# Attention and mixer on one core: the two tail blocks of the token weights in one load, the channel weights of eight steps in pairs of 1024 columns, and k of four units by rows

## The chip, the cores and the metric

The kernel runs on one core of one Trainium2 chip. The time is the device time of one execution in microseconds (us); before the change it is 796.07 (median of three runs, 795.79 to 797.73). Engines are named as the profile names them: PE is TensorE, DVE VectorE, ACT ScalarE, POOL GpSimd, SP SyncE; SPq is SyncE's DMA queue.

## What is computed

Linear attention followed by an MLP mixer. q, k and v have 8 batches, 8 heads, 576 positions and 64 columns.

```python
q_s = softmax(q, over the 64 columns)
k_s = softmax(k, over the 576 positions)
kv  = einsum('bhsd,bhse->bhde', k_s, v)
x   = einsum('bhsd,bhde->bhse', q_s, kv)      # to (8, 576, 512)
h   = relu(x^T @ w_tok1) @ w_tok2             # 576 -> 256 -> 576, over positions
u   = x + h^T
out = u + relu(u @ w_ch1) @ w_ch2             # 512 -> 1536 -> 512, over columns
```

Both softmaxes subtract their maximum first. The four weights are float64.

## The kernel before

A *unit* is one batch and one pair of heads; there are 32, four to a batch. The first eight (n = 0 to 7, `early`) run before the rest: for each, `softmax_k` and `softmax_q`, then `stage_qT`, `stage_kv` (L319, the product k^T v in `kvf`), `stage_y` (L387, w1f times q), `stage_h1` (L395, relu to `hh` and its low part `hl`, L403) and two times `stage_u` (L440 and L422: x and the second token product, in halves of 288 positions). `empty` then takes a half from PSUM into the high and low parts of u, `uh` and `ul` (L434, L435). A high part is the number rounded to the type `fp32r`, the low part what is left; a product of two such pairs takes three matmuls of the four.

After that the work goes by groups of 512 positions and, in each, by twelve steps f of 128 hidden columns: `ch1` (L477, relu(u @ w_ch1)) and `ch2` (L637, times w_ch2). The remaining units are woven in between by the table `put`; the last two groups go through a joint scheme of sums and products.

*k of an early unit.* It is loaded transposed, as `kt`. `softmax_k` takes the maximum over positions (L249), `exp` on ScalarE with that as bias (L253), and five transposes on PE (L256 four whole chunks, L259 the fifth) whose results ScalarE copies to `k_t` (L257, L260). *k of a late unit* (n above 8) is loaded in both layouts: the maximum goes into a column of `dg`, VectorE transposes it in squares of 32 (L265), a DMA writes it to DRAM as `row` (L267), a second one spreads it over all partitions as `mb` (L268), GpSimd subtracts (L278) and ScalarE takes exp (L279). Unit 8 is of a third kind: its maximum is spread by a product with `ones` (L272).

*Weights.* The float64 numbers come as pairs of 32-bit words. `load_weights` loads a block of 128 x 512 and `narrow` makes float32 of it: L201, L203, L204, L206 and L208 on VectorE and L202 on ScalarE; `split` then gives high (L125, ScalarE) and low (L126, VectorE) parts. `load_tok1` and `load_tok2` fill w1f and w2h/w2l, each with a smaller tail block (256 and 128 columns). `load_ch(f)` takes the two blocks of step f; steps 0 to 3 are called inside the loop over the early units, 4 to 11 inside the first channel steps.

What sets the order: the program is written with tiles, and a scheduler with a model of the time orders the instructions of each engine and of each queue; each engine then works its own list in order. `issue_after` (in the code `behind`) keeps a piece out of the lists until a named instruction is in. `early`, `stg` and `cv` are pools with two or three buffers, so a load waits until the buffer's last reader is done.

## Time and profile before

| | |
|---|---|
| median of three runs | 796.07 us |
| the profiled execution | 796.4 us |
| its span, first to last instruction | 794.5 us |
| TensorE's mean granted clock | 0.994 |
| PE busy | 779.0 us (98%) |
| DVE busy | 526.7 us (66%) |
| ACT busy | 326.5 us (41%) |
| POOL busy | 85.1 us (11%) |

The busy time says how much of the span an engine has work in hand. A share over the whole span hides stages, so the windows and timelines of a few stretches stand beside it. Where an engine is full, an instruction costs the time from its start to the next one's start, which is less than its own duration.

### The profile page before, as it was taken

The numbers are of one execution on the slowest core, as the hardware profiler recorded it, in microseconds if no ns is written. First come the engines' busy times: TensorE is split into PE (matmuls) and PEld (weight loads), VectorE is DVE, ScalarE is ACT, GpSimd is POOL, SyncE is SP. The second block draws the span as 40 slices with busy tenths as digits, with TensorE's granted clock in tenths as the row PEclk, the third lists the DMA queues.
The fourth block names the chain that finished last, engine by engine and source line by source line (L and its number), as shares of the span: only waits on it lengthen the run. The fifth ranks groups of instructions, "written<-read, shape, count | busy, mean of one in ns | idle before, by whom it ended". The sixth has DMA issues, their size and how long they took to land.

```text
span 794.5 us, 12177 instructions
## 1 busy us (share of the span) xinstructions
PE 779.0 (98%) x4478; PEld 650.9 (82%) x4478; DVE 526.7 (66%) x1208; ACT 326.5 (41%) x824; POOL 85.1 (11%) x77
## 2 busy tenths in 40 slices
PE   6899999999999999999999999999999999999998
PEld 6688888887888888888888888888888888888886
DVE  6899998897777445755575455564668558975441
ACT  6876544435553343344433434333434413232100
POOL 1000010003122111120201101111111000000020
PEclk8899999999999999999999999999999999999999
DMA  9753422334334221513141212313240000000011
GB/s 289 249 175 104 143 91 101 112 89 133 83 92 137 66 72 37 152 37 100 38 120 54 81 57 74 111 38 85 51 125 18 1 1 28 26 1 0 1 67 40
DMA packets 64786, 65.08 MB, mean 82 GB/s; under 512 B 41944, under 2 KB 45272, under 8 KB 64728
## 3 DMA queue, kind: packets, MB, share of 16 engines
...
## 4 chain that ended last, share of the span: by engine, by line
PE 87%; DVE 6%; ACT 3%; DMA 2%; issue 1%; POOL 1%; DVEq 0%; POOLq 0%; ACTq 0%
PE ps_o L637 30%; PE ps_h L477 26%; PE ps_h L586 7%; PE ps_h L387 6%; PE ps_h L422 5%; PE ps_h L637 4%; PE ps_h L319 2%; PE ps_h L456 2%; PE ps_h L395 1%; ACT q_t L292 1%; DMA q_t<-in_q 1%; PE ps_o L422 1%; DVE stack L374 1%; PE ps_o L387 1%; DVE st L286 0%
## 5 line engine op out<-in xcount | busy, mean ns | idle before, releaser
L637 PE MATMUL ps_o<-h2h,cw 128*128 128x512 f32 x768 | 226.6, 391 | 0.0
L477 PE MATMUL ps_h<-uh,cw 128*128 128x512 f32 x672 | 210.4, 393 | 0.0
L637 PEld LDWEIGHTS ps_o<-h2h,cw 128*128 128x128 f32 x768 | 142.5, 188 | 29.8 <-issue 0.4
L481 DVE SCALAR_TENSOR_TENSOR h2l<-ps_h,h2h 128x512 fp32r<-128x512 f32 x84 | 57.8, 688 | 153.2 <-ACT h2h L480 152.6
L477 PEld LDWEIGHTS ps_h<-uh,cw 128*128 128x128 f32 x672 | 123.7, 188 | 24.4 <-issue 0.4
L637 PE MATMUL ps_o<-h2l,cw 128*128 128x512 f32 x384 | 137.4, 390 | 0.0
L477 PE MATMUL ps_h<-ul,cw 128*128 128x512 f32 x336 | 130.9, 390 | 0.0
L480 ACT ACTIVATE h2h<-ps_h 128x512 fp32r<-128x512 f32 x84 | 49.9, 594 | 90.5 <-PE ps_h L477 80.0
L126 POOL TENSOR_TENSOR ql<-q_t,qh 128x640 fp32r<-128x640 f32 x24 | 39.5, 1647 | 425.6 <-ACT qh L125 390.4
L637 PEld LDWEIGHTS ps_o<-h2l,cw 128*128 128x128 f32 x384 | 72.0, 188 | 15.1
L477 PEld LDWEIGHTS ps_h<-ul,cw 128*128 128x128 f32 x336 | 63.1, 188 | 13.4
L374 DVE COPY stack<-cv_s 32x128 f32<-32x128 f32 (+1 forms) x264 | 55.7, 229 | 3.5 <-PE ps_h L456 0.6
L278 POOL TENSOR_TENSOR k_t<-k_t,mb 128x640 f32<-128x640 f32 x24 | 37.9, 1579 | 109.8 <-DMA mb<-row 78.7
L279 ACT ACTIVATE k_t<-k_t 128x640 f32<-128x640 f32 x24 | 17.7, 739 | 66.2 <-POOL k_t L278 66.2
L495 DVE TENSOR_TENSOR ul<-ps_h,ul 128x512 f32<-128x512 f32 x40 | 27.3, 687 | 24.1 <-PE ps_h L586 23.7
L374 ACT COPY stack<-cv_s 32x160 f32<-32x160 f32 (+1 forms) x120 | 37.4, 311 | 2.8 <-DVE cv_s L364 1.5
L434 ACT CAST uh<-ps_h 128x288 fp32r<-128x288 f32 (+8 forms) x84 | 25.1, 317 | 27.2 <-PE ps_h L456 22.6
L297 ACT ACTIVATE q_t<-q_t 128x640 f32<-128x640 f32 x28 | 20.7, 740 | 32.0 <-DVE q_t L296 31.9
L422 PE MATMUL ps_h<-w2h,hh 128*128 128x288 f32 x112 | 33.7, 302 | 0.0
L422 PE MATMUL ps_h<-w2l,hh 128*128 128x288 f32 x112 | 33.3, 298 | 0.0
L637 PE MATMUL ps_h<-cw 128*128 128x512 f32 x144 | 33.0, 389 | 0.0
L422 PE MATMUL ps_h<-w2h,hl 128*128 128x288 f32 x112 | 32.6, 296 | 0.0
...
## 6 DMA issues: line engine op xcount, KB each, us to landing
stg<-in_w SPq DMA_DIRECT2D x28, 512.0 KB, 3.3
...
mb<-row SPq DMA_DIRECT2D x23, 64.0 KB, 2.9
```

The costliest lines, as they stand in the source:

```text
L126: return lo_eng.tensor_tensor(lo, src, f32(hi), op=ALU.subtract).ins
L278: nc.gpsimd.tensor_tensor(kx, kx, mb.unsqueeze(1).broadcast_to([P, C1, P]), op=ALU.subtract)
L374: eng(stack[row : row + Q, h, 0:n, at : at + Q], turned[x * Q : (x + 1) * Q, 0:n, y * Q : (y + 1) * Q])
L387: nc.tensor.matmul(y[:, 0:TOK], a, w, start=(i == 0), stop=(i == len(mm) - 1))
L422: nc.tensor.matmul(t[:, 0:W], a, w, start=start and i == 0, stop=stop and i == len(mm) - 1)
L434: nc.scalar.copy(uh, src).ins,
L477: nc.tensor.matmul(t, cw[f][x][:, n, :], w, start=(i == 0), stop=(i == 3 * NJ - 1))
L480: nc.scalar.activation(hh, t, AF.Relu).ins,
L481: nc.vector.scalar_tensor_tensor(hl, t, 0.0, f32(hh), op0=ALU.max, op1=ALU.subtract).ins,
L495: nc.vector.tensor_tensor(t, a, b, op=op)
L586: nc.tensor.matmul(t, x(n), w[n], start=(n == 0 and i == 0), stop=(n == 1 and i == 2))
L637: nc.tensor.matmul(to, cw[f][x][:, n0 + n, :], w, start=(first and i == 0), stop=(last and i == 2))
```

## The change

1. **Joint tail.** The tail blocks of w_tok1 (256 columns) and w_tok2 (128) lie in one block and are loaded and narrowed together, 384 columns, into `tails`.
2. **Pairs.** Both blocks of a step f = 0 to 7 go into one raw tile `two` of 1024 columns with two DMAs and are narrowed and split by operations over 1024 columns. The loads are kept behind the issue of a unit's q load (`loaded`), the narrowing behind a unit's multiplication of q by its reciprocal sums (`ready`). Steps 8 to 11 stay as they were.
3. **k by rows for units 5 to 8.** `NATURAL = 5`: these are loaded in both layouts and take the path by `row` and `mb`. For 5 to 7 VectorE subtracts, behind the unit's `ready`, and the row's DMA stands behind the unit's q load; for 8 GpSimd subtracts. Their transposes on PE, and unit 8's product with `ones`, go.

```diff
-        if not u["early"]:
+        if n >= NATURAL:
             nc.sync.dma_start(t.rearrange("p c d -> p (c d)"), k[n])
...
+    def load_two(at, bt, loaded, begun):
+        pool, place = two[0]
...
+        raw = pool.tile([P, 2 * CW, 2], U32, name="two")
+        with behind(loaded):
+            for x, i in enumerate((at, bt)):
+                nc.sync.dma_start(raw[:, x * CW : (x + 1) * CW, :].rearrange("p n w -> p (n w)"), wt[i].bitcast(U32))
+        return narrow(raw, 2 * CW, None, place.tile([P, 2 * CW], U32, name="two_s"), begun)
+
+    def narrow(raw, n, out, s=None, begun=()):
...
-        load_weights(AT_TAIL, TOK, out=w1t)
+        load_weights(AT_TAIL, TOK + NT * TL, out=tails)
...
-        t = load_weights(AT_TAIL + 1, NT * TL).rearrange("p (n t) -> p n t", n=NT)
+        t = tails[:, TOK:].rearrange("p (n t) -> p n t", n=NT)
...
-    def load_ch(f):
+    def load_ch(f, loaded=(), begun=()):
+        if two:
+            t = load_two(AT_C1 + f, AT_C2 + f, loaded, begun).rearrange("p (x n m) -> p x n m", x=2, n=NJ)
+            hi, lo = (cw_rows[f][:, :, y : y + 3 : 2, :].rearrange("p n x m -> p x n m") for y in range(2))
+            narrowed[:] = [split(hi, lo, t, nc.vector)]
+            return
...
-        through = u["n"] > NE
+        through = u["n"] >= NATURAL
...
-        if u["early"]:
+        if u["n"] < NATURAL:
...
-            nc.sync.dma_start(row, dg[0:P:Q, Q : 2 * Q])
+            with behind(u["loaded"] if u["early"] else []):
+                nc.sync.dma_start(row, dg[0:P:Q, Q : 2 * Q])
...
-        nc.gpsimd.tensor_tensor(kx, kx, mb.unsqueeze(1).broadcast_to([P, C1, P]), op=ALU.subtract)
-        nc.scalar.activation(kx, kx, AF.Exp)
+        with behind(u["ready"] if u["early"] else []):
+            eng = nc.vector if u["early"] else nc.gpsimd
+            eng.tensor_tensor(kx, kx, mb.unsqueeze(1).broadcast_to([P, C1, P]), op=ALU.subtract)
+            nc.scalar.activation(kx, kx, AF.Exp)
...
+        u["ready"] = [ready] if u["n"] < NJ else [ready, taken]
...
-            load_ch(n - (NE - F_HEAD))
+
+            f = n - (NE - F_HEAD)
+            load_ch(f, units[min(2 * f + 5, NE - 1)]["loaded"], units[min(f + 5, NE - 1)]["ready"])
```

The new line numbers are 1 to 35 higher: L249 is L274, L387 L416, L395 L424, L403 L432, L422 L451, L440 L469, L477 L506, L201 to L208 are L221 to L228, L126 is L129, L278 is L306.

How the lists of three engines move. First PE, before, at the products of the last two early units (hh_1000 is unit 6's; kvf1_140 unit 7's): the products with unit 6's hh, then the first channel step.

```order
L440 MATMUL ps_o_1055<-qt_963,kvf1_140 128x288
L395 MATMUL ps_h_1048<-kvf1_140,ys_995 128x128 x2
L440 MATMUL ps_h_1065<-qt_963,kvf1_140 128x288
L422 MATMUL ps_h_1004<-w2h_102,hh_1000 128x288
L422 MATMUL ps_h_1004<-w2l_103,hh_1000 128x288
L422 MATMUL ps_o_1014<-w2h_102,hh_1000 128x288
L422 MATMUL ps_o_1014<-w2l_103,hh_1000 128x288
L477 MATMUL ps_h_1122<-uh0_105,cw0_122 128x512 x2
L477 MATMUL ps_h_1122<-ul0_109,cw0_122 128x512
```

Its last quarter, and behind it the rest of unit 6's products with hl_1001:

```order
L477 MATMUL ps_h_1122<-uh0_105,cw0_122 128x512 x2
L477 MATMUL ps_h_1122<-ul0_109,cw0_122 128x512
L422 MATMUL ps_h_1004<-w2h_102,hl_1001 128x288
L422 MATMUL ps_h_1004<-w2h_102,hh_1000 128x288
L422 MATMUL ps_h_1004<-w2l_103,hh_1000 128x288
```

PE in the new order, the end of unit 6's products (hl_964 is now its hl) and what follows:

```order
L451 MATMUL ps_o_977<-w2h_102,hh_963 128x288
L451 MATMUL ps_o_977<-w2l_103,hh_963 128x288
L451 MATMUL ps_o_977<-w2h_102,hl_964 128x288
L424 MATMUL ps_h_1001<-kvf1_147,ys_958 128x128 x2
L469 MATMUL ps_o_1008<-qt_926,kvf1_147 128x288
L469 MATMUL ps_h_1018<-qt_926,kvf1_147 128x288
L506 MATMUL ps_h_1067<-uh0_105,cw0_123 128x512 x2
L506 MATMUL ps_h_1067<-ul0_109,cw0_123 128x512
```

All products of unit 6, those with its hl too, now stand ahead of the first channel step, and unit 7's h1 and kvf products between them.

DVE before, up to hl of unit 6 (hl_1001):

```order
L435 TENSOR_TENSOR ul1_110<-ps_o_919,uh1_106 128x288
L435 TENSOR_TENSOR ul1_110<-ps_h_929,uh1_106 128x160
L206 SCALAR_TENSOR_TENSOR stg_1026<-stg_1026 128x512
L203 SCALAR_TENSOR_TENSOR cv_s_1039<-stg_1037,cv_s_1039 128x512
L435 TENSOR_TENSOR ul2_111<-ps_h_929,uh2_107 128x128
L208 TENSOR_TENSOR cv_s_1028<-stg_1026,cv_s_1028 128x512
L403 SCALAR_TENSOR_TENSOR hl_1001<-ps_o_997,hh_1000 128x256
L204 TENSOR_SCALAR stg_1037<-stg_1037 128x512
L206 SCALAR_TENSOR_TENSOR stg_1037<-stg_1037 128x512
L126 TENSOR_TENSOR cw0_122<-cv_s_1028,cw0_122 128x4x128
```

DVE now, up to hl of unit 6 (hl_964); two_914 and two_989 are the raw weights of f=1 and f=2:

```order
L228 TENSOR_TENSOR two_s_917<-two_914,two_s_917 128x1024
L223 SCALAR_TENSOR_TENSOR two_s_992<-two_989,two_s_992 128x1024
L464 TENSOR_TENSOR ul2_111<-ps_h_902,uh2_107 128x128
L353 TENSOR_SCALAR rs_947<-ps_o_936 128x1
L129 TENSOR_TENSOR cw0_123<-two_s_917,cw0_123 128x2x4x128
L224 TENSOR_SCALAR two_989<-two_989 128x1024
L432 SCALAR_TENSOR_TENSOR hl_964<-ps_o_960,hh_963 128x256
L354 RECIPROCAL rs_947<-rs_947 128x1
L226 SCALAR_TENSOR_TENSOR two_989<-two_989 128x1024
L221 TENSOR_SCALAR two_s_1033<-two_1030 128x1024
```

hl stands behind operations of 1024 columns of two steps, where there were some of 512 columns of one.

SP's queue before, from the weights of f=0 (stg_826, stg_837) past q of units 3 and 4 (q_t_448, q_t_549) to q of unit 5 (q_t_642) and the weights of f=1 on both sides of it (stg_941, stg_952):

```order
L193 DMA stg_826<-in_w 128x1024
L193 DMA stg_837<-in_w 128x1024
L153 DMA q_t_448<-in_q 128x640
L153 DMA q_t_549<-in_q 128x640
L150 DMA kt_t_640<-in_kt 128x640
L193 DMA stg_941<-in_w 128x1024
L180 DMA v_t_86<-in_v 128x4x64 x2
L182 DMA v_t_86<-in_v 32x2x64 x2
L153 DMA q_t_642<-in_q 128x640
L193 DMA stg_952<-in_w 128x1024
```

SP's queue now, at q of units 3 and 4 (q_t_446, q_t_547); stg_1310 is the first block of f=8:

```order
L184 DMA v_t_143<-in_v 128x4x64 x2
L186 DMA v_t_143<-in_v 32x2x64 x2
L197 DMA stg_1310<-in_w 128x1024
L157 DMA q_t_446<-in_q 128x640
L157 DMA q_t_547<-in_q 128x640
```

And a little further, from v of unit 4 to the broadcast of unit 5's maximum (mb_113):

```order
L184 DMA v_t_86<-in_v 128x4x64 x2
L186 DMA v_t_86<-in_v 32x2x64 x2
L154 DMA kt_t_726<-in_kt 128x640
L157 DMA q_t_640<-in_q 128x640
L293 DMA row_646<-dg_108 4x32
L211 DMA two_814<-in_w 128x1024 x2
L161 DMA k_t_642<-in_k 128x640
L294 DMA mb_113<-row_646 128x128
```

One weight load stands ahead of q of units 3 and 4 where two stood; behind q of unit 5 (q_t_640) stand its row, both loads of f=0, its k, and then the broadcast.

## Rows read from the trace of the kernel before

**Rows 1.** The page, part 1: busy us, share of the span and instructions of each engine.

```profile
PE 779.0 (98%) x4478; PEld 650.9 (82%) x4478; DVE 526.7 (66%) x1208; ACT 326.5 (41%) x824; POOL 85.1 (11%) x77
```

**Rows 2.** The waits of PE over the whole span: tile and line that waited, what released it, us in total, times, longest.

```profile
PE ps_h L256 <- ACT kt_t L253: 3.5, 2, 2.4
PE ps_o L395 <- ACT ys L389: 2.1, 1, 2.1
...
PE ps_h L387 <- ACT w1f L222: 1.0, 1, 1.0
PE ps_h L319 <- ACT k_t L279: 0.7, 1, 0.7
```

**Rows 3.** The windows: for each stretch its length, the busy us (and instructions) of PE, PEld, DVE, ACT and POOL, then the granted TensorE clock (1.00 is full), the DMA engines' share and GB/s.

```profile
25.00:30.00 5.00, 2.06 (x11) 1.21 (x9) 4.87 (x13) 4.94 (x15) 0.00 (x0) 1.00 0.95 304
30.00:35.00 5.00, 4.88 (x38) 4.25 (x39) 3.40 (x8) 3.07 (x10) 0.00 (x0) 0.66 0.69 245
...
60.00:70.00 10.00, 10.00 (x81) 8.92 (x80) 10.00 (x27) 6.96 (x19) 0.00 (x0) 1.00 0.27 80
70.00:80.00 10.00, 10.00 (x73) 8.74 (x72) 8.66 (x22) 6.20 (x17) 0.00 (x0) 1.00 0.40 122
```

**Rows 4.** The timeline of PE around the transposes of one unit's kt (L256 four chunks, L259 the fifth): start us, duration us, engine, line, operation, out<-in.

```profile
55.04 0.60 PE L256 MATMUL ps_o<-ident,kt_t 128*128 128x128 f32 x4
55.48 0.27 PE L259 MATMUL ps_h<-ident,kt_t 128*128 128x128 f32 x1
55.59 0.60 PE L349 MATMUL ps_o<-ident,q_t 128*128 128x128 f32 x4
```

**Rows 5.** The timeline of DVE (VectorE), same columns; the time from one start to the next is what an operation costs while the engine is full. An operation of 512 columns with two inputs (L206) and one of 640 (L301); one of 512 with a single input (L201); one of 1024 columns with two inputs (L126).

```profile
45.06 0.69 DVE L206 SCALAR_TENSOR_TENSOR stg<-stg 128x512 f32<-128x512 uint32 x1
45.66 0.82 DVE L301 TENSOR_TENSOR q_t<-q_t,st 128x640 f32<-128x640 f32 x1
46.40 0.81 DVE L298 TENSOR_REDUCE st<-q_t 128x10 f32<-128x640 f32 x1
...
69.95 0.41 DVE L201 TENSOR_SCALAR cv_s<-stg 128x512 uint32<-128x512 uint32 x1
70.29 0.14 DVE L325 RECIPROCAL rs<-rs 128x1 f32<-128x1 f32 x1
...
89.39 1.22 DVE L126 TENSOR_TENSOR w1l<-w1f,w1h 128x1024 fp32r<-128x1024 f32 x1
90.52 0.69 DVE L206 SCALAR_TENSOR_TENSOR stg<-stg 128x512 f32<-128x512 uint32 x1
```

**Rows 6.** The timeline of SPq, the DMA issues of SyncE: start us, duration us of the issue, line, out<-in; x2 are two issues in a row. The last two are of unit 9.

```profile
25.03 1.08 SPq L193 DMA_DIRECT2D stg<-in_w  x2
27.22 0.80 SPq L153 DMA_DIRECT2D q_t<-in_q  x2
...
37.10 0.35 SPq L153 DMA_DIRECT2D q_t<-in_q  x1
...
170.91 0.62 SPq L267 DMA_DIRECT2D row<-dg  x1
172.75 0.33 SPq L268 DMA_DIRECT2D mb<-row  x1
```

**Rows 7.** The timeline of DVE at the maxima of q of units 3 and 4, with the idle time ahead of each and what ended it.

```profile
32.17 0.82 DVE L286 TENSOR_REDUCE st<-q_t 128x10 f32<-128x640 f32 x1 [1.28 <-DMA q_t<-in_q]
...
33.81 0.82 DVE L286 TENSOR_REDUCE st<-q_t 128x10 f32<-128x640 f32 x1 [0.28 <-DMA q_t<-in_q]
```

**Rows 8.** The timeline of PE at the first h1 of unit 0, with the wait ahead of it.

```profile
30.12 0.71 PE L395 MATMUL ps_o<-kvf,ys 128*128 128x128 f32 x4 [2.06 <-ACT ys L389]
```

**Rows 9.** The timeline of PE at h1 of unit 6 (L395), the products of its kvf (L440), the first channel step (L477) and the products with hl behind that (L422).

```profile
74.64 0.61 PE L395 MATMUL ps_o<-kvf,ys 128*128 128x128 f32 x4
75.08 0.65 PE L440 MATMUL ps_h<-qt,kvf 128*128 128x288 f32 x2
75.57 1.13 PE L440 MATMUL ps_o<-qt,kvf 128*128 128x288 f32 x4
...
78.00 0.62 PE L477 MATMUL ps_h<-uh,cw 128*128 128x512 f32 x2
...
80.75 0.29 PE L422 MATMUL ps_h<-w2h,hl 128*128 128x288 f32 x1
80.88 0.30 PE L422 MATMUL ps_h<-w2h,hh 128*128 128x288 f32 x1
```

**Rows 10.** The timeline of DVE at two pieces of ul (L435) and at hl of unit 6 (L403).

```profile
74.41 0.31 DVE L435 TENSOR_TENSOR ul<-ps_h,uh 128x160 fp32r<-128x160 f32 x1
74.64 0.68 DVE L206 SCALAR_TENSOR_TENSOR stg<-stg 128x512 f32<-128x512 uint32 x1
...
76.65 0.41 DVE L403 SCALAR_TENSOR_TENSOR hl<-ps_o,hh 128x256 fp32r<-128x256 f32 x1
76.98 0.42 DVE L204 TENSOR_SCALAR stg<-stg 128x512 uint32<-128x512 uint32 x1
```

**Rows 11.** The page, part 6: DMA issues by tile, KB each, median us from issue to landing.

```profile
stg<-in_w SPq DMA_DIRECT2D x28, 512.0 KB, 3.3
...
mb<-row SPq DMA_DIRECT2D x23, 64.0 KB, 2.9
```

More of the change, by code (lines that the diff above doesn't have):

```diff
@@ L140, in attn_mixer_kernel @@
     conv = [(stg, cv)]
+    two = []
     def load_unit(b, j):
@@ L194, in load_weights @@
         return narrow(raw, n, out)
-    def narrow(raw, n, out):
+    def load_two(at, bt, loaded, begun):
+        pool, place = two[0]
+        if not wide:
+            t = place.tile([P, 2 * CW], F32, name="two_s")
+            for x, i in enumerate((at, bt)):
+                nc.sync.dma_start(t[:, x * CW : (x + 1) * CW], wt[i])
+            return t
+        raw = pool.tile([P, 2 * CW, 2], U32, name="two")
+        with behind(loaded):
+            for x, i in enumerate((at, bt)):
+                nc.sync.dma_start(raw[:, x * CW : (x + 1) * CW, :].rearrange("p n w -> p (n w)"), wt[i].bitcast(U32))
+        return narrow(raw, 2 * CW, None, place.tile([P, 2 * CW], U32, name="two_s"), begun)
+    def narrow(raw, n, out, s=None, begun=()):
         w0, w1 = raw[:, 0:n, 0], raw[:, 0:n, 1]
-        s = conv[-1][1].tile([P, C1 * P], U32, name="cv_s")[:, 0:n]
-        nc.vector.tensor_scalar(s, w1, 20, 0x7FF, op0=ALU.logical_shift_right, op1=ALU.bitwise_and)
+        if s is None:
+            s = conv[-1][1].tile([P, C1 * P], U32, name="cv_s")[:, 0:n]
+        with behind(begun):
+            nc.vector.tensor_scalar(s, w1, 20, 0x7FF, op0=ALU.logical_shift_right, op1=ALU.bitwise_and)
         nc.scalar.activation(s, s, AF.Relu, bias=ebias, scale=2.0**23)
@@ L296, in softmax_q @@
             nc.vector.tensor_tensor(qt, qt, st[:, 0, :].unsqueeze(2).broadcast_to([P, G, D]), op=ALU.subtract)
-            nc.scalar.activation(qc, qc, AF.Exp)
+            taken = nc.scalar.activation(qc, qc, AF.Exp).ins
             nc.vector.tensor_reduce(st[:, 1, :], qt, axis=AX.X, op=ALU.add)
@@ L300, in softmax_q @@
         nc.vector.reciprocal(st[:, 2, :], st[:, 1, :])
[L301 removed]
+        ready = nc.vector.tensor_tensor(qt, qt, st[:, 2, :].unsqueeze(2).broadcast_to([P, G, D]), op=ALU.mult).ins
+        u["ready"] = [ready] if u["n"] < NJ else [ready, taken]
         if u["early"]:
@@ L687, in soft @@
             softmax_q(units[n])
+            if NATURAL <= n <= NE:
+                exp_k(units[n])
     def pe_stages(n):
@@ L711, in attn_mixer_kernel @@
     stg_more = early_pools.enter_context(tc.tile_pool(name="stg_more", bufs=2))
+    two_pools = [early_pools.enter_context(tc.tile_pool(name=x, bufs=2)) for x in ("two", "two_s")]
     conv[:] = [(stg, cv), (stg_more, cv)]
+    two[:] = [two_pools]
     w1f = early1.tile([P, C1, TOK], F32, name="w1f")
-    w1t = early1.tile([P, TOK], F32, name="w1t")
+    tails = early1.tile([P, TOK + NT * TL], F32, name="tails")
+    w1t = tails[:, 0:TOK]
     v_ring.append(v_tile(early1))
@@ L761, in attn_mixer_kernel @@
     more_pools = ExitStack()
-    stg_more = more_pools.enter_context(tc.tile_pool(name="stg_more", bufs=2))
-    cv_more = more_pools.enter_context(tc.tile_pool(name="cv_more", bufs=2))
-    conv[:] = [(stg, cv), (stg_more, cv_more)]
+    conv[:] = [(stg, cv)]
+    two[:] = [[more_pools.enter_context(tc.tile_pool(name=x, bufs=2)) for x in ("two", "two_s")]]
     unit_banks[0] = (ph,)
@@ L845, in attn_mixer_kernel @@
                 more_pools.close()
-                conv[:] = [(stg, cv)]
+                two.clear()
                 ch_rows(F_MORE, NF)
@@ L919, in pieces @@
     cut += list(w_tok2[:, : C * P].reshape(NT, P, CW))
-    tail = np.zeros((2, P, CW), w_tok1.dtype)
+    tail = np.zeros((1, P, CW), w_tok1.dtype)
     tail[0, :, :TOK] = w_tok1[rows_and_columns(S)[0][C * P :]]
-    tail[1, :, : NT * TL] = w_tok2[:, C * P :].reshape(NT, P, TL).transpose(1, 0, 2).reshape(P, NT * TL)
+    tail[0, :, TOK : TOK + NT * TL] = w_tok2[:, C * P :].reshape(NT, P, TL).transpose(1, 0, 2).reshape(P, NT * TL)
     cut += list(tail)
```

10 lines of the change are left out of this document (6 added, 4 removed).

## The prediction

> **What bounds the kernel now.** I read four views in this order. The busy times come first: TensorE (PE) is busy for 779.0 of the span's 794.5 us, VectorE for 526.7 [rows 1]. What PE doesn't fill is little, and its waits say where: on kt's exp 3.5 and on ys 2.1 us, on w1f 1.0, and 0.7 on the exp of a late unit's k [rows 2]. The windows show that nearly all of it lies in the first 45 us; from 60 to 80 us PE is busy for 10.00 of every 10 us, while VectorE is at 10.00 and 8.66 there [rows 3]. So a gain has to be PE work taken away or a wait of the head, and beside the head VectorE is the one engine with so little room that the change can turn it into a wait. The timelines below give durations and the times at which work comes ready. All durations are from one profiled execution (796.4 us beside the median of 796.07, so 0.3 above it); differences are made against its own time.
>
> **The change, part by part.**
>
> *PE work taken away.* Units 5, 6 and 7 lose their five transposes of kt each. In the timeline the four of a unit's whole chunks and the fifth hold PE from 55.04 to 55.48 and on to 55.59, that is 0.55 us [rows 4]; three units give 1.65. Where PE is full this comes straight off its queue. Unit 8 loses the product of 128 x 128 that spread its maximum, priced as the fifth transpose, 0.11, and at most twice that. Sum: 1.8 us less for PE.
>
> *The joint tail.* One load and five or six small VectorE operations go, but 128 columns more pass ahead of w1f's last chunk, and the scheduler now puts one 512-column operation of w2 ahead of it too. A 512-column operation with two inputs takes 0.60 us from start to start, one with a single input 0.34 [rows 5]. The 512-column one costs 0.60, and 128 columns in three operations of the former kind and two of the latter cost 3 x 0.15 + 2 x 0.08, some 0.6: w1f is ready about 1.2 us later. In exchange VectorE's q of units 3 and 4, for which it now waits 1.28 and 0.28 us until 32.17 and 33.81, is less late: their loads go out at 27.22 behind two weight loads issued at 25.03 [rows 6, 7], and in the new order one weight load stands there, with the two for f=4, 5 gone from further ahead as well; 1.5 MB less, so I put q3 and q4 at about 31.1 and 31.9, 1 to 2 us earlier. PE starts its first h1 at 30.12, after 2.06 us of waiting for ys [rows 8]; with w1f later it starts at about 31.2, but with unit 3's kt and unit 2's q transposed inside that wait, and the rest of the head is no longer held by q3 and q4. Where the head ends, at 45 us, PE then stands 0.5 to 2.2 us earlier. Which end holds depends on its clock.
>
> After PE was busy for only 2.06 of 5 us its clock is granted at 0.66 in the next 5 us, in which it fell to the lower of its levels, 1.2 GHz, for a part; it was 1.00 before [rows 3]. That stretch costs 1.7 us: 5 us at 0.66 do the work of 3.3. The lower end, 0.5, keeps that loss, the upper one, 2.2, lacks it. The Trainium skill ("TensorE: Matmul & The Clock Gate", HAM oscillation and PE-mode transpose) has the clock fall across waits, and it adds that a transpose doesn't count as busy for it in the way of a matmul. By that rule the transposes moved into the wait would not hold the clock, and the lower end is the one to take. The windows here can't separate transposes from other matmuls, so I keep both ends in the range.
>
> *Weights in pairs.* A step's two blocks were ten VectorE operations of narrowing and two of splitting, at 512 columns: 2 x (4 x 0.60 + 2 x 0.34), 6.2 us. The trace has one operation at 1024 columns, 1.13 us from start to start against 2 x 0.60 [rows 5]; so each merged operation saves 0.07, a step 0.4 at most. That changes little; what matters is the order. VectorE works its queue in order, and the longest operation that can stand ahead of something due grows from 0.60 to 1.13.
>
> *k by rows, VectorE's side.* The maximum stays; a 32x32 transpose is added, of 32 columns, which I put at 0.15 (between nothing and the 0.34 of 512 columns with one input), and a subtraction over 640 columns with two inputs, as the 0.74 of q's [rows 5]. Units 5 to 7 thus add 3 x 0.9 = 2.7 us to an engine that is full from 60 to 70 [rows 3]. ScalarE loses two copies for each and isn't the limit.
>
> *Where that goes.* The place is the second group of token products of unit 6. Now its h1 stands at 74.64 and its hl comes from VectorE at 76.65; PE meanwhile takes the first channel step at 78.00, and the products with hl wait behind it until 80.75 [rows 9, 10]. So hl has 4 us of room. In the new order all of unit 6's products stand ahead of that first channel step, and what filled the gap is behind them. PE reaches hl's first product at 78.00 less what now stands behind it (an h1 of 0.44 and two kvf products of 0.49 [rows 9], 1.42) less the 1.65 of transposes less the head's 0.5 to 2.2: 72.7 to 74.4. VectorE gets there as follows. From q of unit 5 (its load goes out at 37.10 now [rows 6], after the wait for a free buffer; I put its landing at 40.8, between 40.0 and 41.5) 70 operations stand ahead of hl. At 1024 columns there are seven with two inputs and six with one, 7 x 1.13 + 6 x 0.64 = 11.8 (0.64 is an estimate, twice 0.34 less 0.04), and the low parts of two steps, 2 x 1.13 = 2.3; three subtractions of k make 2.2, thirteen operations on q and one maximum 14 x 0.74 = 10.3. Four earlier hl at 0.33 and fourteen pieces of ul, 0.23 for one of 160 columns and 0.3 on the mean [rows 10], make 5.4, and seventeen tiny ones at about 0.1 make 1.7. That is 33.7 us: hl is begun at 74.5 and there at 74.9, between 74.0 and 75.6. So PE waits there for about 1.4 us (0 to 2.9). After it come eight products at 0.13 [rows 9] and the 1.42: the first channel step starts at 77.4, and the point that answers to it is 79.05 now. The gain is 1.65 (0.9 to 2.5); for the passing on of a semaphore and the like I take 1.5. What the head gained beyond that is lost at this wait: VectorE decides, not PE.
>
> *Row and broadcast DMAs, and SyncE's queue.* For unit 5 SyncE now issues q5's load, the row, 1 MB of weights, k5, and then the broadcast. A late unit's pair of row and broadcast has 1.84 us between issues [rows 6], and a broadcast lands 2.9 us after its issue, a weight load of 512 KB 3.3 [rows 11]. So the row goes at about 39.2, the broadcast at 41.2, and behind 1 MB it lands at about 45; VectorE comes to the subtraction at about 47.3 to 48.9. Two to four us of cover; for units 6 and 7, 3 to 7. If that is gone, VectorE stands, and its whole queue with it (see the third rival).
>
> *Later.* The weights of f=0 to f=11 come ready 5 to 15 us before their matmuls by the same addition, unit 8's k more than 50 us, and behind unit 8 PE's order is the old one. The 0.7 before unit 9 stays. So nothing there is gained or lost.
>
> Sum: 1.8 of PE's work and the head's 0.5 to 2.2 (1.3), against them 1.4 to 1.6 of waiting at hl: 1.5 us less, 794.9 on the profiled execution and 794.6 on the median.
>
> **The rivals.**
>
> *All of it is kept.* If q5 lands at 40 or sooner, or VectorE's queue is shorter by 1.5 us than I add up, hl is there when PE asks, and transposes and head count in full: 2.4 to 4.0 us, 792.8 as its middle. For it: VectorE in the trace has a few waits that an earlier q takes away [rows 7]. Against: it is at 10.00 of 10 from 60 to 70 already [rows 3].
>
> *VectorE eats the gain.* With hl done at 76.5 or later the wait takes all that PE saved: 796.0. It needs the 33.7 us to be 1.6 too few, 5%. The Trainium skill ("Perfetto Trace Analysis", Optimizing Scalar/DVE Operations) says that where VectorE isn't saturated but makes others wait, breaking operations up lets work come sooner; joining them is the opposite. By that rule each due result stands up to 0.5 us longer behind a 1024-column operation, and one such delay at hl would leave 1.0 of the 1.5, 795.1: inside my range. No row of before shows it.
>
> *The broadcast is late (slower).* SyncE takes its queue in order, and q5's load, which waits for a free buffer, holds all of them. If the broadcast lands after about 48.5, VectorE stands at the subtraction, and every us there arrives at hl as a us for PE. Up to 1.5 us late only eats the gain; beyond 4 late, 799 and more. For it: in the head transfers overrun their medians (q3 lands 4.9 after its issue [rows 6, 7]). Against: 2 to 4 us of cover, and DMA is less loaded after 35 us.
>
> **How the numbers follow.** A measurement of this kernel can tell about 0.3%, 2.4 us, from no change. The forecast (gain 0.3 to 2.4) has a chance of 0.52, all kept 0.27, VectorE eats it 0.13, the late broadcast 0.08. The first and third are no change, the second is faster by over 0.3% nearly always, the fourth slower: 0.27, 0.65, 0.08. The range goes from 792.0, the far end of all kept, to 797.8, a broadcast that is late by some 3 us; beyond it lie the worse half of the fourth and a tenth at the fast side.
>
> **What would show it.** Right: PE has no transposes of kt for units 5 to 7, waits 1 to 2 us for VectorE's hl of unit 6 shortly before its first channel step, and that step starts at about 77.5. VectorE doesn't wait for the broadcast. Wrong: no wait at hl (then the first rival, with the step at 76 or before), a first step at 79 or later, VectorE idle ahead of its subtraction of k, or a difference that arises behind 190 us, where I see no cause.

## The result, and the profile after

The changed kernel takes 802.72 us (median of 6 runs, 801.38 to 805.31) against 796.34 (6 runs, 795.79 to 797.73): a ratio of 1.0082, with a 95% interval of 1.0069 to 1.0094. It is slower by 6.4 us, where 1.5 us of gain were forecast, and lies outside the range. The profiled execution took 801.38, its span is 799.6, 5.1 more than before.

PE's waits from 50 to 200 us, from its timeline, with the start of the first channel step, 78.93 (start us, duration us, engine, line, operation, out<-in, and in brackets the idle time ahead and what ended it):

```profile
54.10 0.80 PE L348 MATMUL ps_o<-v_t,k_t 128*64 128x65 f32 x18 [0.85 <-ACT ys L418]
...
62.14 0.80 PE L348 MATMUL ps_h<-v_t,k_t 128*64 128x65 f32 x20 [0.46 <-ACT k_t L307]
...
76.57 0.40 PE L451 MATMUL ps_h<-w2h,hl 128*128 128x288 f32 x1 [0.96 <-DVE hl L432]
...
78.93 0.83 PE L506 MATMUL ps_h<-uh,cw 128*128 128x512 f32 x2
...
138.75 0.73 PE L506 MATMUL ps_h<-uh,cw 128*128 128x512 f32 x2 [0.64 <-DVE cw L129]
...
162.67 2.12 PE L666 MATMUL ps_o<-h2h,cw 128*128 128x512 f32 x8 [1.56 <-ACT h2h L509]
...
189.75 0.80 PE L348 MATMUL ps_h<-v_t,k_t 128*64 128x65 f32 x20 [2.14 <-ACT k_t L307]
```

(h2h and h2l are the high and low parts of a channel step's relu(u @ w_ch1).) The kernel before had three waits of 0.3 us or more behind 50 us: 0.31 at 251, 0.37 at 273, and at unit 9's k

```profile
185.37 0.80 PE L319 MATMUL ps_h<-v_t,k_t 128*64 128x65 f32 x20 [0.73 <-ACT k_t L279]
```

Now PE waits 0.85, 0.46 and 0.96 at the early units, 0.64 for the weights of f=7, 1.56 for the result of a channel step and 2.14 for unit 9's k. Up to the end of the early units the account is even: after all their products and 9 matmuls of the second channel step PE stands at 85.55, where the kernel before stands at 83.40 with these 9 (2.04 us) still to do, so 0.1 later now. Ahead of the wait for unit 9's k it is 3.0 later (187.61 against 184.64), of which the waits of 0.64 and 1.56 are 2.2 and some 0.7 are not located; at 197 us it is 6.0, from 316 us on 5.0, and 5.1 at the end.

The windows of the changed kernel (length, busy us of PE, PEld, DVE, ACT, POOL, granted clock, DMA share, GB/s) show the two places that decide:

```profile
60.00:70.00 10.00, 9.46 (x75) 8.39 (x74) 10.00 (x23) 7.15 (x19) 0.00 (x0) 1.00 0.46 143
...
70.00:80.00 10.00, 9.04 (x65) 7.32 (x64) 9.65 (x16) 7.28 (x16) 0.00 (x0) 1.00 0.31 107
...
90.00:100.00 10.00, 10.00 (x46) 8.29 (x45) 5.73 (x8) 3.51 (x4) 0.00 (x0) 1.00 0.91 341
...
185.00:190.00 5.00, 2.86 (x20) 2.05 (x20) 4.95 (x11) 4.56 (x13) 3.07 (x2) 1.00 0.31 100
...
190.00:195.00 5.00, 5.00 (x40) 4.55 (x36) 4.32 (x14) 0.72 (x3) 0.00 (x0) 0.66 0.54 135
```

From 60 to 80 us PE is no longer full (10.00 of 10 in [rows 3]). From 90 to 100 VectorE is busy for 5.73 us; in the kernel before it was 10.00:

```profile
90.00:100.00 10.00, 10.00 (x46) 8.29 (x45) 10.00 (x18) 3.92 (x7) 0.00 (x0) 1.00 0.72 247
```

After the wait for unit 9's k, with 2.86 busy of 5, PE's clock is granted at 0.66 for the next 5 us, as in the head of the kernel before [rows 3]; by PE's positions before and after that stretch (4.4 and 6.0 us later than before) that is another 1.6 us.

VectorE at the early units and in that gap, from its timeline:

```profile
47.14 0.82 DVE L274 TENSOR_REDUCE dg<-kt_t 128x1 f32<-128x640 f32 x1 [1.74 <-DMA kt_t<-in_kt]
...
49.22 0.82 DVE L306 TENSOR_TENSOR k_t<-k_t,mb 128x640 f32<-128x640 f32 x1
...
76.10 0.41 DVE L432 SCALAR_TENSOR_TENSOR hl<-ps_o,hh 128x256 fp32r<-128x256 f32 x1
...
92.61 0.69 DVE L510 SCALAR_TENSOR_TENSOR h2l<-ps_h,h2h 128x512 fp32r<-128x512 f32 x1 [1.34 <-ACT h2h L509]
...
94.64 0.69 DVE L221 TENSOR_SCALAR two_s<-two 128x1024 uint32<-128x1024 uint32 x1 [1.34 <-DMA two<-in_w]
...
96.61 1.23 DVE L223 SCALAR_TENSOR_TENSOR two_s<-two,two_s 128x1024 uint32<-128x1024 uint32 x1 [1.28 <-ACT two_s L222]
...
137.47 1.23 DVE L129 TENSOR_TENSOR cw<-two_s,cw 128x1024 fp32r<-128x1024 f32 x1 [1.12 <-ACT cw L128]
```

Its queue stood at 47.14 for kt of unit 7, so the subtraction of unit 5's k began at 49.22. From q of unit 5 (41.16) to hl of unit 6 (76.10) it is busy for 33.2 of 34.9 us, and this is its one wait. In 91 to 97 us it stood three times: for a channel step's result, for the raw words of f=4, and for ScalarE's part of them. SyncE's queue tells why (start, duration of the issues; x4 are four in a row):

```profile
38.41 0.86 SPq L211 DMA_DIRECT2D two<-in_w  x2
...
39.32 0.43 SPq L161 DMA_DIRECT2D k_t<-in_k  x1
...
40.97 0.46 SPq L154 DMA_DIRECT2D kt_t<-in_kt  x1
...
73.07 0.84 SPq L211 DMA_DIRECT2D two<-in_w  x2
...
89.62 1.75 SPq L211 DMA_DIRECT2D two<-in_w  x4
```

kt of unit 7 goes out at 40.97 behind the 1 MB of f=0 and k of unit 5, and VectorE has it 6.2 us later; the median from issue to landing of these loads was 3.3 in the kernel before. Behind the pair of f=3, issued at 73.07, nothing leaves the queue until the four loads of f=4 and 5 go out from 89.62 on: their buffers lie where the early units' tiles were.

ScalarE then shows how a late weight reaches PE, and GpSimd how it reaches unit 9:

```profile
50.06 0.74 ACT L307 ACTIVATE k_t<-k_t 128x640 f32<-128x640 f32 x1 [2.83 <-DVE k_t L306]
...
53.70 0.35 ACT L418 COPY ys<-ps_o 128x256 f32<-128x256 f32 x1
...
161.41 0.72 ACT L222 ACTIVATE cv_s<-cv_s,ebias 128x512 uint32<-128x512 uint32 x1 [2.54 <-DVE cv_s L221]
...
162.04 0.58 ACT L509 ACTIVATE h2h<-ps_h 128x512 fp32r<-128x512 f32 x1
...
184.68 0.40 ACT L463 CAST uh<-ps_h 128x288 fp32r<-128x288 f32 x1 [4.37 <-PE ps_h L485]
...
184.98 0.73 ACT L128 CAST qh<-q_t 128x640 fp32r<-128x640 f32 x1
```

```profile
185.84 1.57 POOL L129 TENSOR_TENSOR ql<-q_t,qh 128x640 fp32r<-128x640 f32 x1 [65.40 <-ACT uh L463]
...
187.37 1.54 POOL L306 TENSOR_TENSOR k_t<-k_t,mb 128x640 f32<-128x640 f32 x1
```

At 50.06 exp of unit 5's k comes after 2.83 us of waiting for the subtraction, and ys (L418), which PE waits for at 54.10, is queued behind it. At 161.41 ScalarE has waited 2.54 us for VectorE's first operation on a block of f=11 (which had itself waited 0.83 us for the block's load), and h2h (L509), which PE waits for, stands behind. At unit 9 the rounding of q (L128) stands behind a copy of u that waits 4.37 us for PE; the kernel before had it at 179.30, ahead of its copies of u (182.38). GpSimd's two operations and exp follow, and PE gets k at 189.75.

### The profile page after: what moved, and what is told of

It is laid out like the page before. It is cut to its first block, busy times and chain, and to the rows that moved or that the text cites. A ratio compares the mean times of both kernels' runs of the same rounds, so it can differ in the third digit from the quotient of the medians.

```text
span 799.6 us, 12073 instructions
## 1 busy us (share of the span) xinstructions
PE 779.8 (98%) x4461; PEld 650.5 (81%) x4461; DVE 528.1 (66%) x1159; ACT 321.8 (40%) x799; POOL 84.1 (11%) x78
## 4 chain that ended last, share of the span: by engine, by line
PE 80%; DVE 11%; DMA 4%; ACT 3%; issue 1%; SPq 0%; DVEq 0%; ACTq 0%
PE ps_o L666 28%; PE ps_h L506 24%; PE ps_h L615 7%; PE ps_h L416 6%; PE ps_h L451 5%; PE ps_h L666 4%; PE ps_h L348 2%; PE ps_h L485 2%; PE ps_h L424 1%; DMA two<-in_w 1%; DMA kt_t<-in_kt 1%; ACT q_t L320 1%; DVE cw L129 1%; DMA stg<-in_w 1%; DVE two L226 1%
## 5 line engine op out<-in xcount | busy, mean ns | idle before, releaser
L506 PE MATMUL ps_h<-uh,cw 128*128 128x512 f32 x672 | 211.9, 394 | 0.6 <-DVE cw L129 0.6
L506 PEld LDWEIGHTS ps_h<-uh,cw 128*128 128x128 f32 x672 | 124.1, 189 | 25.7 <-DVE cw L129 1.1
L666 PE MATMUL ps_o<-h2l,cw 128*128 128x512 f32 x384 | 135.6, 390 | 0.0
L506 PE MATMUL ps_h<-ul,cw 128*128 128x512 f32 x336 | 131.2, 391 | 0.0
L509 ACT ACTIVATE h2h<-ps_h 128x512 fp32r<-128x512 f32 x84 | 49.9, 594 | 90.6 <-PE ps_h L506 86.9
L129 POOL TENSOR_TENSOR ql<-q_t,qh 128x640 fp32r<-128x640 f32 x24 | 38.4, 1598 | 354.3 <-ACT qh L128 244.6
L506 PEld LDWEIGHTS ps_h<-ul,cw 128*128 128x128 f32 x336 | 63.2, 188 | 13.4
L403 DVE COPY stack<-cv_s 32x128 f32<-32x128 f32 (+1 forms) x264 | 57.5, 236 | 2.9
L306 POOL TENSOR_TENSOR k_t<-k_t,mb 128x640 f32<-128x640 f32 x24 | 38.0, 1585 | 187.1 <-DVE cw L129 107.1
L307 ACT ACTIVATE k_t<-k_t 128x640 f32<-128x640 f32 x27 | 20.0, 740 | 62.7 <-POOL k_t L306 59.8
L403 ACT COPY stack<-cv_s 32x160 f32<-32x160 f32 (+1 forms) x120 | 37.3, 311 | 1.2
L451 PE MATMUL ps_h<-w2h,hl 128*128 128x288 f32 x112 | 32.9, 300 | 1.0 <-DVE hl L432 1.0
L451 PE MATMUL ps_h<-w2h,hh 128*128 128x288 f32 x112 | 33.7, 302 | 0.0
L451 PE MATMUL ps_h<-w2l,hh 128*128 128x288 f32 x112 | 33.1, 297 | 0.0
L464 DVE TENSOR_TENSOR ul<-ps_h,uh 128x288 fp32r<-128x288 f32 (+8 forms) x84 | 29.1, 349 | 4.2 <-ACT uh L463 3.3
```

The lines of the kernel that those rows point to most:

```text
L129: return lo_eng.tensor_tensor(lo, src, f32(hi), op=ALU.subtract).ins
L306: eng.tensor_tensor(kx, kx, mb.unsqueeze(1).broadcast_to([P, C1, P]), op=ALU.subtract)
L403: eng(stack[row : row + Q, h, 0:n, at : at + Q], turned[x * Q : (x + 1) * Q, 0:n, y * Q : (y + 1) * Q])
L451: nc.tensor.matmul(t[:, 0:W], a, w, start=start and i == 0, stop=stop and i == len(mm) - 1)
L464: nc.vector.tensor_tensor(ul, src, f32(uh), op=ALU.subtract).ins,
L506: nc.tensor.matmul(t, cw[f][x][:, n, :], w, start=(i == 0), stop=(i == 3 * NJ - 1))
```

## The experiments

Each ratio is that of a kernel's runs to runs of the kernel before on the same chip; what a run gives back is the difference of two ratios, times 796 us (the changed kernel's 1.0082 is 6.5 us). The theory at the start (T): the words of f=4 come late, VectorE's gap puts off all later weights, and PE waits for them. Its rivals: k by rows costs it (K), or the length of the joined operations (W).

**f=4 to 7 in single blocks again.**

```diff
-    conv[:] = [(stg, cv)]
-    two[:] = [[more_pools.enter_context(tc.tile_pool(name=x, bufs=2)) for x in ("two", "two_s")]]
+    stg_more = more_pools.enter_context(tc.tile_pool(name="stg_more", bufs=2))
+    cv_more = more_pools.enter_context(tc.tile_pool(name="cv_more", bufs=2))
+    conv[:] = [(stg, cv), (stg_more, cv_more)]
+    two.clear()
...
```

> The changed kernel with one part undone: the weights of steps f=4 to 7 are loaded and narrowed in blocks of 512 columns from the pools of before; f=0 to 3 stay in pairs, joint tail and k by rows stay. Theory T (late weights): the time is lost behind 90 us, because the raw words of f=4 may be loaded only when the early units' memory is free, VectorE stands from 91 to 97 us (5.73 us busy of 10 from 90 to 100, 10.00 before) and is late from there on (PE waits 0.64 at 138.75, 1.56 at 162.67, 2.14 at 189.75, and then gets a clock of 0.66 for 5 us). It expects about 797 (795.5 to 798.5), VectorE above 9 of 10 in 90 to 100, and no wait of PE over 0.9 us behind 100. Rival K (k by rows costs it: the chain row, broadcast, subtraction, and the new order at units 8 and 9): 801 to 803 as it is. Rival W (the length of 1024-column operations holds due results up wherever weights are narrowed): half of it goes, 799 to 800.

797.06 us, 1.0016 (1.0007 to 1.0025): 5.3 us of the 6.5 are back. VectorE from 90 to 100:

```profile
90.00:100.00 10.00, 10.00 (x46) 8.29 (x45) 9.70 (x19) 6.11 (x10) 0.00 (x0) 1.00 0.72 248
```

The waits at f=7, at f=11 and at unit 9's k are gone; one of 1.35 us stands at 181.91, and the three at the early units stay (1.07, 0.47, 0.98). The time is the one that T gave; that no wait over 0.9 us would stand behind 100 was wrong. This run undoes the late pool and the long operations of f=4 to 7 together.

**Pools of their own for the pairs**, apart from the early units' memory:

```diff
+    more_pools = ExitStack()
+    two_pools = [more_pools.enter_context(tc.tile_pool(name=x, bufs=2, side="right")) for x in ("two", "two_s")]
     early_pools = ExitStack()
...
-    two_pools = [early_pools.enter_context(tc.tile_pool(name=x, bufs=2)) for x in ("two", "two_s")]
...
```

The line that opens the second pair of pools for f=4 to 7 goes too.

> The changed kernel with its pairs in place for all of f=0 to 7, but the pools of the raw and narrowed pairs are one and the same for both stretches and lie apart from the early units' memory, so that f=4's words wait only for a buffer. Theory T (late weights, see late_single): VectorE's gap from 91 to 97 us goes, f=4's first operation comes before 88 instead of 94.64, and the time falls to about 797 (795.5 to 798.5). Rival K (k by rows): 801 to 803. Rival W (length of the operations): 801 to 803, since every operation is as long as before.

800.36, 1.0053 (1.0036 to 1.0070). VectorE is busy for 10.00 of 10 us from 90 to 100; f=4's loads go out at 82.28 (89.62 in the changed kernel), it is split at 102.7 us (110.7), and the waits for f=7 and at unit 9's k are gone, so the place of the pool is shown to make the gap. But only 2.3 us came back, and the time lies outside the ranges of T, K and W. PE now waits later (the profiled execution took 798.48, the other three 800.0 and more):

```profile
154.30 0.73 PE L666 MATMUL ps_o<-h2l,cw 128*128 128x512 f32 x2 [0.39 <-DVE h2l L510]
...
160.21 0.50 PE L666 MATMUL ps_o<-h2l,cw 128*128 128x512 f32 x1 [0.62 <-DVE h2l L510]
...
163.84 2.12 PE L666 MATMUL ps_o<-h2h,cw 128*128 128x512 f32 x8 [1.30 <-ACT h2h L509]
```

**Each part alone.**

```text
 pairs_only        joint tail and k by rows undone (NATURAL = NE, through for n > NE)
 rows_only         pairs and joint tail undone
 tail_only         pairs and k by rows undone
 late_pairs_only   as pairs_only, f=0 to 3 in blocks of 512 columns
 early_pairs_only  as pairs_only, f=4 to 7 in blocks of 512 columns
```

> The kernel before with the pairs of f=0 to 7 alone: no joint tail, k of units 5 to 8 as before. Theory T: all of the loss and no gain from transposes, 800 to 802, with VectorE's gap in 90 to 100. Rival K: 796 to 797, as before. Rival W: 799 to 802.

> The kernel before with k by rows for units 5 to 8 alone: no pairs, no joint tail. Theory T: PE's 1.8 us of transposes are gained, less waits of up to 1.3 us in the head: 794.5 to 796. Rival K: 800 to 803. Rival W: 794.5.

> The kernel before with the joint tail alone. Theory H (w1f is ready about 1.2 us later and PE starts its first h1 later, partly given back by q of units 3 and 4): 795.5 to 797.5. Rival: the joint tail holds up the whole head: 798 or more.

> The kernel before with pairs for f=4 to 7 alone (f=0 to 3 in blocks of 512 columns, no joint tail, k as before). Theory T (f=4 to 7 come late, because their pairs may be loaded only when the early units' memory is free): it holds all of what the pairs cost, 798 to 800, VectorE's gap at 91 to 97 us is there, and f=7 is split after 135 us (128.2 before). Rival E (the pairs of f=0 to 3 cost it, by the wait at unit 6's hl): 796 to 797.

> The kernel before with pairs for f=0 to 3 alone (f=4 to 7 in blocks of 512 columns, no joint tail, k as before). Theory T: 796 to 797, as before; f=7 split before 131 us. Rival E: 798 to 800, with a wait of over 1 us at hl.

Pairs alone: 798.70, 1.0025 (1.0015 to 1.0034). Rows alone: 799.00, 1.0031 (1.0020 to 1.0042). Tail alone: 796.87, 1.0011 (1.0001 to 1.0021). Late pairs: 797.25, 1.0014 (1.0004 to 1.0023). Early pairs: 798.40, 1.0025 (1.0016 to 1.0035). Only the tail falls where it was expected. The pairs lie under the ranges of T and W and over K's, the rows miss all three of theirs, late pairs fall between T and E, and for early pairs E holds, against T. No part gains anything alone, k by rows least of all: PE saves its transposes and waits elsewhere. Where, from their timelines of PE, rows_only first and late_pairs_only next (each profile is of the longest of that kernel's runs, 800.91 and 798.62 us):

```profile
56.07 0.66 PE L378 MATMUL ps_o<-ident,q_t 128*128 128x128 f32 x4 [1.15 <-DVE q_t L329]
...
65.12 0.63 PE L378 MATMUL ps_h<-ident,q_t 128*128 128x128 f32 x4 [1.75 <-issue]
...
164.95 0.73 PE L506 MATMUL ps_h<-uh,cw 128*128 128x512 f32 x2 [1.14 <-DVE cw L129]
```

```profile
44.21 1.09 PE L378 MATMUL ps_o<-ident,q_t 128*128 128x128 f32 x4 [3.71 <-ACT kt_t L278]
```

In rows_only q of an early unit comes late, the profile shows no cause for 1.75 us at 65.12, and late weights hold PE up for 1.14 us at 164.95; the clock is granted at 0.71 from 65 to 70. In late_pairs_only VectorE is busy for 9.78 of 10 from 90 to 100, since f=0 to 3 in single blocks still fill it, f=7 is split at 128.5 (T wanted it after 135), and no wait stands behind 50 us; the pairs of f=4 to 7 cost little there by themselves. It is their coming after pairs of f=0 to 3, done by 90 us, that opens the gap. pairs_only has both: VectorE is busy for 7.24 of 10, f=7 is split at 137.6 and f=11 at 166.9, about 1 us sooner than in the changed kernel, and no wait stands behind 90 us. PE comes to f=7 there at 141.01, behind twelve products with w_ch2 from 138.29 on; in the changed kernel's list f=7 comes ahead of these, and PE asks for it at 138.1. So the cost of late weights hangs on PE's list too. Its one wait of 0.3 us or more behind 50 us is that for hl, 1.35 us at 82.69. early_pairs_only has the wait at hl (1.35 us at 83.12), and 0.44 before it; f=7 is split at 132.7 (T: before 131). Every part makes the scheduler write other lists, and each list has waits of its own.

**The length of the operations.**

```diff
+        for x in range(2):
+            narrow(raw[:, x * CW : (x + 1) * CW, :], CW, None, s[:, x * CW : (x + 1) * CW], begun)
...
+            for x in range(2):
+                narrowed[:] = [split(cw[f][2 * x], cw[f][2 * x + 1], t[:, x], nc.vector)]
```

> The changed kernel with its loads, pools and places of the pairs, but every narrowing and splitting operation on 512 columns again, two where there was one. Theory T (late words): f=4 to 7 stay late and the time stays at 801 to 804. Rival W (the length of 1024-column operations holds due results up): 797 to 799, with the wait at unit 6's hl gone.

799.71, 1.0038 (1.0023 to 1.0053), between the two: 3.5 us back, which speaks for W, but the wait at unit 6's hl is 1.32 us there, longer than the 0.96 that W wanted to go. VectorE's gap is smaller (7.26 of 10 busy), but f=7 and f=11 are split as late as in the changed kernel (139.4 and 167.4) without a wait of PE at either; PE's list has f=7 at 141.31 here too, behind twelve products with w_ch2. It tells W and T apart only in part.

**The subtraction on GpSimd**, in late_single:

```diff
-            eng = nc.vector if u["early"] else nc.gpsimd
+            eng = nc.gpsimd
```

> The kernel late_single (f=4 to 7 in blocks of 512 columns, the rest as changed) with the subtraction of k of units 5 to 7 on GpSimd, which takes 2.2 us off VectorE before unit 6's hl. Theory V (VectorE's full queue eats the gain of the transposes): the wait of 0.98 at hl goes, 795.5 to 796.5. Rival: GpSimd's subtraction takes 1.58 us where VectorE's takes 0.74, so k comes later where PE already waits 0.47 for it, and nothing is gained: 797 to 798.

802.93, 1.0076 (1.0061 to 1.0091). The wait at hl is gone, but PE waits for the exp of an early unit's k, and later for a channel step:

```profile
65.06 0.66 PE L378 MATMUL ps_h<-ident,q_t 128*128 128x128 f32 x4 [3.03 <-ACT k_t L307]
...
168.52 1.19 PE L666 MATMUL ps_o<-h2l,cw 128*128 128x512 f32 x4 [1.71 <-DVE h2l L510]
```

Behind the first wait the clock is 0.66 from 65 to 70. Neither expectation reached so far: the mechanism is the rival's, the size is several times its own. Less work on VectorE doesn't help when the result that PE needs next comes later.

**Where the second limit lies.** The waits of keep_pool at 154 to 164 us led to another theory (S): the blocks of f=8 to 11 pass through two raw buffers, and what comes before only decides how late they begin. These kernels leave out half of the weights of f=8 to 11, so their result is another.

```diff
+            if f >= F_MORE:
+                t = load_weights(at + f, CW // 2).rearrange("p (n m) -> p n m", n=NJ // 2)
+                for y in (slice(0, 2), slice(2, 4)):
+                    narrowed[:] = [split(cw[f][x][:, y, :], cw[f][x + 1][:, y, :], t, nc.vector)]
+                continue
```

> The kernel keep_pool (pairs with pools of their own) in which the weights of f=8 to 11 are only half loaded and narrowed: 256 columns of each block, copied into both halves of its place, so the products of those steps have other weights. Theory S (a second limit: the blocks of f=8 to 11 pass through two raw buffers, one step takes about 9 us, and PE, when it comes sooner, only waits for f=11): the waits of 0.39, 0.62 and 1.30 us at 154 to 164 us go, and the time falls by 2 to 3 us against keep_pool (800.4), to 797.5 to 798.5. Rival: these waits come from ScalarE's and VectorE's order (h2h and h2l behind other work) and stay: 800.

> The kernel before with the same half weights of f=8 to 11. Theory S: PE comes just in time for f=11 there, so nothing changes: 795.5 to 797. If the limit of the raw buffers costs the kernel before something as well, it falls by 1 us or more.

> The changed kernel with only half of the weights of f=8 to 11 loaded and narrowed (256 columns of each block, copied into both halves of its place; the products of those steps have other weights). If f=8 to 11 are what carries the loss behind 90 us (theory S, two raw buffers, about 9 us a step, now begun later), the wait of 1.56 us at 162.67 and what follows it at unit 9 (2.14 us, the clock at 0.66) go, and only the 0.64 for f=7 stays: 796 to 798. If the late words of f=4 to 7 act in another way (theory T without S): 800 to 802.

> The kernel late_single (f=4 to 7 in blocks of 512 columns) with the same half weights of f=8 to 11. By theory S late_single is hardly held up by f=8 to 11 (it has no wait at 154 to 165 us), so it gains 1 us or less over late_single (797.06): 796 to 797. A gain of 2 us or more would mean that the limit holds back that kernel too, and that PE's saved transposes are lost there.

keep_pool with half weights: 795.38 (0.9994, 0.9984 to 1.0004), 4.7 us less, more than S expected. The kernel before: 795.32 (0.9991, 0.9981 to 1.0001), no change that can be told. The changed kernel: 795.51 (1.0001, 0.9983 to 1.0019), 6.4 us less, again more; the waits for f=7, f=11 and unit 9's k are all gone. late_single: 795.57 (0.9990, 0.9981 to 1.0000), 2.1 less, faster than its range; given the intervals that can't be told from 1 us. So nothing of the loss behind 90 us is left once f=8 to 11 are half as much work. Half the weights are half the loads and half of VectorE's operations on them, and f=8's operations stand between those of f=7; so these runs don't separate the raw buffers from VectorE's amount of work. The end of each step's splitting (second block, VectorE, us):

| | f=4 | f=5 | f=6 | f=7 | f=8 | f=9 | f=10 | f=11 |
|---|---|---|---|---|---|---|---|---|
| before | 104.0 | 116.2 | 122.8 | 128.2 | 138.7 | 147.7 | 157.0 | 164.8 |
| changed | 110.7 | 122.1 | 132.2 | 138.7 | 140.7 | 149.2 | 158.7 | 167.5 |
| late_single | 108.6 | 116.7 | 128.1 | 132.4 | 139.0 | 147.7 | 156.1 | 163.9 |

f=8 to 11 follow each other by 8 to 10 us in all three, and 10 us of delay at f=7 are 2 to 3 at f=11.

**f=4 alone in single blocks.**

```diff
-        if two:
+        if two and f != F_HEAD:
```

> The changed kernel with f=4 alone in blocks of 512 columns through the two raw buffers that are free early; f=5 to 7 stay in pairs in the late pool. Theory T (the late words of f=4 leave VectorE idle from 91 to 97 us and shift all that follows): most of the loss behind 90 us goes, 797.5 to 800, f=7 split before 136 us. Rival G (something else of the pairs of f=4 to 7, their number of buffers or their order): 801 to 804.

800.06, 1.0049 (1.0035 to 1.0062): 2.6 of the 6.5 us back, and just outside T's range. f=4 is split at 102.8, but f=7 at 136.6, and 1.34 us of waiting for f=11 stay at 163.12. VectorE waits for f=5's pair there (1.66 us at 100.89). T holds for f=4 and not for the whole loss, since f=5 meets the same late pool.

**Once more, unchanged.**

> The changed kernel once more, unchanged, for a second profile. If the waits behind 130 us (f=7's weights, h2h behind the weights of f=11, unit 9's k) belong to the kernel, they are there again within 0.5 us each. If they are an accident of the one profiled execution, others stand in their place.

> The kernel before once more, for a second profile: no wait over 0.8 us behind 50 us, 795 to 797, and the clock of the head (0.50 from 15 to 20 us, 0.66 from 30 to 35) to compare.

The changed kernel: 806.61, one execution. The same places behind 130 us wait, the first longer by 1.6 us and the second shorter by 0.9 than in the first profile, against 0.5 expected, and the first and the last with a lower clock behind them:

```profile
143.46 0.73 PE L506 MATMUL ps_h<-uh,cw 128*128 128x512 f32 x2 [2.23 <-DVE cw L129]
...
167.95 2.11 PE L666 MATMUL ps_o<-h2h,cw 128*128 128x512 f32 x8 [0.70 <-ACT h2h L509]
...
195.01 0.80 PE L348 MATMUL ps_h<-v_t,k_t 128*64 128x65 f32 x20 [2.14 <-ACT k_t L307]
```

```profile
145.00:150.00 5.00, 5.00 (x17) 3.95 (x16) 4.28 (x10) 1.93 (x3) 0.00 (x0) 0.67 0.00 0
...
195.00:200.00 5.00, 4.99 (x39) 4.64 (x40) 4.57 (x15) 0.48 (x2) 0.00 (x0) 0.66 0.53 132
```

VectorE's wait for kt of unit 7 is 2.95 us here (1.74 in the first profile), and the one for f=4's words 2.65 (1.34). A wait of PE of 1.62 us at 51.42, for another unit's hl, is new. The order on ScalarE at unit 9 is that of the first profile, q behind the copy of u, and so is the copy's wait, 4.37 us. The kernel before: 795.99, with waits of at most 0.60 behind 50 us.

**f=0's pair one unit later**, in late_single:

```diff
-            load_ch(f, units[min(2 * f + 5, NE - 1)]["loaded"], units[min(f + 5, NE - 1)]["ready"])
+            load_ch(f, units[min(f + 6, NE - 1)]["loaded"], units[min(f + 5, NE - 1)]["ready"])
```

> The kernel late_single with the load of f=0's pair put behind unit 6's q, not unit 5's, so that kt of unit 7 goes out ahead of that 1 MB. Theory Q (SyncE's queue: VectorE waits 1.74 us at 47.14 for kt of unit 7, which stands behind the pair; the subtraction of k, ScalarE's exp behind it and ys come late, and PE waits 0.85 to 1.07 us at 54): that wait and the one of PE at 54 go, and the time falls by 1 us against late_single (797.06), to 795.5 to 796.5, where it would be level with the kernel before or a little ahead. Rival: another load takes its place (unit 6's broadcast, now behind the pair), and the time stays at 796.5 to 798.

797.91, 1.0022 (1.0011 to 1.0033). VectorE no longer waits for kt of unit 7, nor PE at 54 us, as theory Q has it; but VectorE waits for the pair itself, and PE at another unit's hl (VectorE first, then PE):

```profile
53.88 0.69 DVE L221 TENSOR_SCALAR two_s<-two 128x1024 uint32<-128x1024 uint32 x1 [1.87 <-DMA two<-in_w]
```

```profile
69.88 0.40 PE L451 MATMUL ps_o<-w2h,hl 128*128 128x288 f32 x1 [1.23 <-DVE hl L432]
```

The clock is 0.70 from 70 to 75 us behind that. The rival holds: another load takes its place.

Of these kernels none with all of its weights beats the kernel before.

## Why the prediction was wrong

*PE work taken away* was right in size: PE is busy for 776.8 us in late_single, 2.2 less than before [rows 1] (forecast 1.8). None of it reaches the end.

*The early units.* The place was right, and so was the sum of VectorE's work up to hl: 33.7 us forecast, 33.2 busy. The wait at unit 6's hl was forecast at 1.4 us (0 to 2.9) and is 0.96. But hl was begun at 76.10, 1.6 later than forecast, because VectorE stood for 1.74 us at kt of unit 7; it was done at 76.5, which is the second rival's condition, and as that rival says the gain was gone at the end of the early units (0.1 later than before). The two other waits of PE, 0.85 and 0.46, were not in the sum: for unit 5 I had given VectorE's subtraction a cover of two to four us against the broadcast, and looked at that load alone. The broadcast was in time; kt of unit 7, behind the same 1 MB on SyncE's queue and ahead of the subtraction on VectorE's, was not. It was the third rival's mechanism with another load: single_load6, where that load goes out ahead of the 1 MB, has neither VectorE's wait nor these two. (The 0.46 is at unit 6's k; how it hangs on that load was not followed.) The three add up to 2.27 where 1.4 to 1.6 stood in the sum, and the first channel step started at 78.93, not 77.5. With the transposes of 1.65 that leaves 0.5 to 0.7 for the head, the lower end. The joint tail alone, from which that gain was to come, is 0.9 us slower than before (tail_only, 0.1 to 1.7).

*The head's clock.* I took 1.7 us of low clock as the difference between the head's two ends. The second profile of the kernel before has 30 to 35 us at full clock, where the first had 0.66 [rows 3]. Over all windows of the head the second execution lost 1.7 us (5 us times what the clock lacks, summed) and the first 5.1, and yet the second took 795.99 against 796.4. PE waits in the head for ScalarE either way (2.40 and 2.06 us for exp and ys in the first). The changed kernel has 30 to 35 us at 1.00 and still only the lower end, so the clock didn't choose it. That step priced nothing; that the lower end came out is luck. The rule of the Trainium skill on the clock ("TensorE: Matmul & The Clock Gate", HAM oscillation), that it falls across waits, did bear out later, though the Trainium skill's own example has longer waits: 2.23 us at 143 us (second profile) and 2.14 at 189 were followed by 5 us at 0.67 and 0.66. After 1.56 us at 162.67 it stayed at 1.00.

*Later* is the step that failed: "the weights of f=0 to f=11 come ready 5 to 15 us before their matmuls by the same addition". The addition carried VectorE on as a full engine behind 90 us and took f=4's words as landed. They could not be loaded before the early units' memory was free, so f=7 was split at 138.7, when PE had asked for it at 138.1, and f=11 at 167.5. "The 0.7 before unit 9 stays" failed with it: that wait is 2.14. In late_single and after_half8, where these waits are gone, 5.3 and 6.4 of the 6.5 us are back. In the profile they are 0.64 and 1.56 at the weights, 1.41 more at unit 9 and 1.6 of clock, 5.2 together; with the 0.1 of the early units and the 0.7 not located that is the 6.0 at 197 us, less 0.7 for the two waits of before at 251 and 273 that went, and some 0.2 not located: 5.1 at the end.

That the gap comes from the pool's place is shown by keep_pool. That the loss behind 90 us needs the full work on f=8 to 11 is shown by after_half8. That the gap alone makes it is not shown: keep_pool closes the gap and gives back only 2.3 us, and halves has weights as late, pairs_only nearly so, without a wait of PE for f=7 or f=11. PE's list, written anew for each kernel, decides too, and no run holds it fixed. Unit 9's q stands behind the copy of u in both profiles, so that is the scheduler's order; why it chose it was not tried. keep_pool and late_single don't wait there.

*The rule on breaking up operations* ("Perfetto Trace Analysis", Optimizing Scalar/DVE Operations, of the Trainium skill), by which 795.1 was given: halves went back to 512 columns and took 3.5 us off the changed kernel, so it points the right way, but the wait at hl didn't fall, and the cost isn't where I had it act. VectorE is full (10.00 of 10) from 60 to 70 us, where the Trainium skill speaks of an engine that isn't.
